# Attention beside a plain FFN, reordered per head, and an FFN end in an earlier form

## Chip, core and metric

The kernel runs on one core of one Trainium2 chip. The metric is device time in microseconds (us), the median of several runs. The kernel before takes 1391.65 us, median of three runs between 1391.4 and 1393.33 us. The profile is of one of these executions and has a span of 1389.6 us.

Five engines run in parallel, each through its own list of instructions in order: TensorE (PE in the profile; its weight loads are PEld), VectorE (DVE), ScalarE (ACT), GpSimd (POOL) and SyncE (SP), which here only starts transfers. An engine waits for another through semaphores.

## The reference

Attention with a threshold, then a two-layer network (FFN) with an ELU between its layers. Shapes: 8 batches, 8 heads, 576 positions, 64 values per head; the FFN has 4608 tokens, 512 inputs and 2048 hidden values. All in float32 on the chip.

```python
def _attn_ref(q, k, v, tau):
    scale = 1.0 / np.sqrt(q.shape[-1])
    scores = scale * np.matmul(q, k.transpose(0, 1, 3, 2))
    thresh = np.max(scores, axis=-1, keepdims=True) - tau
    scores = np.where(scores >= thresh, scores, -1000000000.0)
    scores = scores - np.max(scores, axis=-1, keepdims=True)
    attn = np.exp(scores)
    attn = attn / (np.sum(attn, axis=-1, keepdims=True) + 1e-09)
    return np.matmul(attn, v).astype(np.float32)

def _moe_ref(x, w_in, w_out):
    h = x @ w_in
    g = np.where(h > 0.0, h, np.exp(np.minimum(h, 0.0)) - 1.0)
    return (g @ w_out).astype(np.float32)
```

The weights arrive as float64, so the kernel first converts them by integer arithmetic, a piece of 128 x 512 at a time.

## The kernel before

Attention goes in steps: a step is 128 query rows of a pair of heads (or, every fifth step, the tails of both heads as one head's worth). For each step TensorE makes the scores; VectorE takes the row maxima; GpSimd makes from them the exponent's bias `nb` and the threshold `th`; ScalarE takes the exponentials `e`; VectorE masks them with the threshold and sums the rows in the same operation; GpSimd normalizes. Later TensorE transposes the weights and multiplies them with v.

The program has five parts in time: attention of the first batch (to about 107 us); attention beside the first plain FFN, with weight conversion (to about 240 us, of which conversion lasts to about 219 us); attention beside the rest of the plain FFN (to about 314 us); attention beside FFN groups that use seven products in place of eight (to about 1150 us), which come from sums of blocks; and the last two groups alone.

A piece of weights goes through five operations: `convert_rest` and `convert_abs` on ScalarE, `convert_top` and `convert_end` on VectorE, `convert_add` on GpSimd.

```python
    def convert_top(i):          # VectorE, lines 136 and 137
        ...
            nc.vector.tensor_scalar(top, hi, 3, 0x3FFFFFFF, ALU.logical_shift_left, ALU.bitwise_and)
            nc.vector.scalar_tensor_tensor(top, hi, 0xC0000000, top, ALU.bitwise_and, ALU.bitwise_or)
    def convert_add(i):          # GpSimd, line 143
        ...
            nc.gpsimd.tensor_tensor(top, top, staged[i][:, :, 0].bitcast(I32), ALU.add)
    def convert_end(i):          # VectorE, line 155
        ...
            nc.vector.scalar_tensor_tensor(pieces[i][1], mag, 1.125 * 2.0**-15, top, ALU.is_ge, ALU.mult)
```

The softmax of a step, for both heads at once:

```python
    def exponentials(pr, i, hs):
        ...
        nc.vector.tensor_reduce(st["mx"][:, cs], src[:, :, :, :HALF], axis=AX.XY, op=ALU.max)      # 248
        nc.gpsimd.tensor_scalar(st["nb"][:, cs], st["mx"][:, cs], nkeep, 1.0, ALU.mult, ALU.mult)  # 249
        nc.gpsimd.tensor_scalar(st["th"][:, cs], st["mx"][:, cs], 1.0, ntau, ALU.mult, ALU.add)    # 250
        for h in hs:
            e = att.tile([P, 2, HALF], FP32, name="e")
            nc.scalar.activation(e, st[h][:, :, :HALF], AF.Exp, bias=st["nb"][:, h : h + 1], scale=keep)
    def masks(pr, i, hs):
        ...
        for h in hs:
            nc.vector.scalar_tensor_tensor(wv, sc[:, :, :HALF], st["th"][:, h : h + 1], e, ALU.is_ge, ALU.mult,
                                           accum_out=sm[:, h : h + 1])                             # 265
        nc.vector.tensor_scalar(sm[:, cs], sm[:, cs], 1e-9, None, ALU.add)
        nc.vector.reciprocal(rs[:, cs], sm[:, cs])
    def normalize(pr, i, hs):
        for h in hs:
            nc.gpsimd.tensor_scalar(wv, wv, st["rs"][:, h : h + 1], 1.0, ALU.mult, ALU.mult)       # 274
```

In the second part the order is fixed by the program. One step of its loop, in which `now` are the two pieces of weights that are converted, and `ffn_halves(n)` puts n half units of the FFN on TensorE; `finish_units` puts their exponential (ScalarE), `minus` (GpSimd) and ELU (VectorE):

```python
            scores(*step, hs)
            if valued: out_values = values(...)
            parts = turn_parts(*steps[n - 1])
            for x in now[:1]: convert_top(x)
            finish_units(carried, slice(0, 2))
            for x in now[:1]: convert_add(x)
            copies = parts[0]()
            ...
            exponentials(*step, hs)
            finish_units(carried, slice(2, None))
            ...
            for x in now[:1]: convert_abs(x)
            share = SHARES[n % NB]
            after = ffn_halves(share[0])
            finish_units(after, ACT)
            for x in now[1:]: convert_top(x); convert_add(x); convert_abs(x)
            parts[1]()()
            second = ffn_halves(share[1])
            finish_units(second, ACT)
            if len(parts) > 2: parts[2]()()
            carried = ffn_halves(share[2])
            masks(*step, hs)
            finish_units(after + second, slice(1, 2))
            for x in now: convert_end(x)
            finish_units(after + second, slice(2, None))
            normalize(*step, hs)
            if i in (2, 3): (prep_q if i == 2 else prep_k)(pr + 1); ...
```

At the end, a unit of the first layer (`first_product`) is seven quarters on TensorE into three PSUM banks; ScalarE copies a bank (`w`, `u`, `s`), GpSimd and VectorE add, ScalarE takes two exponentials (the second after a lag), and VectorE makes the ELUs. `second_round` is the second layer, fourteen products of two quarters. A step of the agenda is placed at an estimated time, which fixes the order of instructions and nothing else.

Of the kernel before, what the change touches and what calls it, by code (L numbers as in the profile page):

```python
# [19 lines left out]
def kernel(  # L20
# [12 lines left out]
    P = 128  # L33
# [236 lines left out]
    def normalize(pr, i, hs):  # L270
        st = open_steps[pr, i]
        for h in hs:
            wv = st["w"][:, h * S : (h + 1) * S]
            nc.gpsimd.tensor_scalar(wv, wv, st["rs"][:, h : h + 1], 1.0, ALU.mult, ALU.mult)  # L274

# [303 lines left out]
    for name, bufs in (("s", 1), ("f", 2)):  # L579
        psum[name] = banks.enter_context(tc.tile_pool(name=f"ps_{name}", bufs=bufs, space=PSUM))  # L580
# [10 lines left out]
    with tc.manual_schedule():  # L591
# [3 lines left out]
        for n in range(per_seq, SWITCH):  # L595
# [13 lines left out]
            for x in now[:1]:  # L609
                convert_top(x)  # L610
            finish_units(carried, slice(0, 2))
            for x in now[:1]:
                convert_add(x)
# [3 lines left out]
            exponentials(*step, hs)  # L617
# [4 lines left out]
            for x in now[:1]:  # L622
                convert_abs(x)
            share = SHARES[n % NB]
            after = ffn_halves(share[0])
            finish_units(after, ACT)
            for x in now[1:]:
                convert_top(x)
                convert_add(x)
                convert_abs(x)  # L630
            parts[1]()()
            second = ffn_halves(share[1])
            finish_units(second, ACT)
            if len(parts) > 2:
                parts[2]()()
            carried = ffn_halves(share[2])
            masks(*step, hs)
            finish_units(after + second, slice(1, 2))
            for x in now:
                convert_end(x)  # L640
            finish_units(after + second, slice(2, None))
            normalize(*step, hs)
# [19 lines left out]
    apart.append(True)  # L662
    for name, bufs, stack in (("f", 3, ctx), ("s", 2, banks), ("t", 1, banks)):
        psum[name] = stack.enter_context(tc.tile_pool(name=f"ps_{name}2", bufs=bufs, space=PSUM))
# [81 lines left out]
    with tc.manual_schedule():  # L746
# [78 lines left out]
        def first_product(g, u):  # L825
# [69 lines left out]
            def elu(c):  # L895
# [21 lines left out]
                [(0.1, lambda: add(h(1, 1), 0, "s1")), (1.4 if attending[0] else 1.1, lambda: exp(1))],  # L917
# [147 lines left out]
        def ffn_quarters(n):  # L1065
            while n and (quarters or queue):
                if not quarters:
                    f, a = queue.popleft()
                    mine = f(*a)

                    if (f, a) == (second_round, (B, 1)):
                        mine = [mine[x] for x in (0, 2, 6, 1, 3, 4, 5)] + mine[7:]
                    quarters.extend(mine)
                p, posts = quarters.popleft()
                end = on_pe(QT, p)
                for lag, f in posts:
                    at(end + lag, f)
                n -= 1

        def max_of(pr, i, h):  # L1080
            st = open_steps[pr, i]
            nc.vector.tensor_reduce(st["mx"][:, h : h + 1], st[h][:, :, :HALF], axis=AX.XY, op=ALU.max)  # L1082

        def bound_of(pr, i, h):
            st = open_steps[pr, i]
            nc.gpsimd.tensor_scalar(st["th"][:, h : h + 1], st["mx"][:, h : h + 1], 1.0, ntau, ALU.mult, ALU.add)  # L1086

        def exp_of(pr, i, h):
            st = open_steps[pr, i]
            nc.scalar.mul(st["nb"][:, h : h + 1], st["mx"][:, h : h + 1], nkeep)  # L1090
            e = att.tile([P, 2, HALF], FP32, name="e")
            nc.scalar.activation(e, st[h][:, :, :HALF], AF.Exp, bias=st["nb"][:, h : h + 1], scale=keep)  # L1092
            st[h] = st[h], e

        def mask_of(pr, i, h):
            st = open_steps[pr, i]
            if h == 0:
                st["w"] = wpool[0].tile([P, 2 * S], FP32, name="w")
            sc, e = st.pop(h)
            wv = st["w"][:, h * S : (h + 1) * S].rearrange("p (a n) -> p a n", a=2)  # L1100
            nc.vector.scalar_tensor_tensor(wv, sc[:, :, :HALF], st["th"][:, h : h + 1], e, ALU.is_ge, ALU.mult,  # L1101
                                           accum_out=st["sm"][:, h : h + 1])

        def reciprocal_of(pr, i, hs):
            st = open_steps[pr, i]
            cs = slice(hs[0], hs[-1] + 1)
            nc.vector.tensor_scalar(st["sm"][:, cs], st["sm"][:, cs], 1e-9, None, ALU.add)
            nc.vector.reciprocal(st["rs"][:, cs], st["sm"][:, cs])  # L1108
# [67 lines left out]
        attending[0] = False  # L1176
        xs = [late["x"].tile([P, 2, CT], FP32, name=f"x{x}") for x in range(3)]
        for x, f in enumerate(sums_x(B - 1, xs)):
            at(clock[0] + 2.0 + 1.5 * x, f)
        while quarters or queue:  # L1180
            ffn_quarters(1)
            run_extra(0.9)
# [4 lines left out]

        banks.close()
        psum["f"] = ctx.enter_context(tc.tile_pool(name="ps_f3", bufs=5, space=PSUM))
        ends[:] = [bank() for _ in range(5)] + ends  # L1190
# [13 lines left out]
        nc.sync.dma_start(xts[B], xtail.rearrange("j p n -> p j n"))  # L1204
        xs = [qkp.tile([P, S], FP32, name="qT") for _ in range(2)] + [qkp.tile([P, TAIL + S], FP32, name="kT")]
# [49 lines left out]
```

## Time and profile before

| part of the time line (us) | TensorE busy | length |
|---|---|---|
| 106.8 to 218.7, attention with plain FFN and conversion | 95.95 us | 111.9 us |
| 218.7 to 239.6, the same without conversion | 20.88 us | 20.9 us |
| 239.6 to 314, attention with the rest of the plain FFN | 73.23 us | 74.4 us |
| 314 to 1150, attention with the groups of seven products | 829.01 us | 836.0 us |
| 1150 to 1389.6, the end | 227.10 us | 239.6 us |

Some durations of single instructions that are used below: a joint maximum of two heads 1.34 us, of one head 0.75 us; an exponential 0.83 us; a mask 0.82 us; a normalization 0.74 us when nothing else runs beside it, 0.86 us on average; `convert_add` 1.29 us; `convert_end` 0.68 us.

In a row of the time line the columns are start, length, engine, line, operation, what it writes and reads, and in brackets how long the engine stood idle before it and who released it. In the chain of waits each row is a piece of the chain of work that ended last.

### The profile page before, as it was taken

To read this page: it belongs to the slowest core of one execution; us is meant where nothing else is said; L and a number is where in the kernel's file an instruction comes from. 1 tells how busy PE (TensorE), PEld (TensorE's weight loads), DVE (VectorE), ACT (ScalarE), POOL (GpSimd) and SP (SyncE) were. 2 spreads that over 40 slices of the span, in tenths; PEclk is the share of its full clock that TensorE was granted. 3 is DMA by queue.
4 is the path that set the end of the run, shared out by engine and by line. 5 is a ranking of instruction groups with operands and counts; after the bars stand their busy time and mean duration, and the time that the engine had idled before them with its cause. 6 is when DMAs were issued, how large, how long until landed. Compare 5 with 4: busy or idle time off the path is not lost.

```text
span 1389.6 us, 21973 instructions
## 1 busy us (share of the span) xinstructions
PE 1336.3 (96%) x6566; PEld 988.0 (71%) x6566; DVE 1064.0 (77%) x2364; ACT 632.6 (46%) x1387; POOL 827.4 (60%) x1329
## 2 busy tenths in 40 slices
PE   6897989999999999999999999999999999999998
PEld 4454745747777777777777777777777777887886
DVE  6777885988888888888788878887888875444433
ACT  5566665225454445445453545363636351422421
POOL 5567774878657564757475747574766655423423
PEclk9899999999999999999999999999999999999999
DMA  5245452688898989798888888898889785321211
GB/s 114 57 88 146 136 147 44 189 245 239 236 261 234 264 218 256 197 281 231 235 229 259 238 235 235 242 251 220 236 229 273 211 238 146 115 69 54 92 57 31
DMA packets 316343, 259.83 MB, mean 187 GB/s; under 512 B 208320, under 2 KB 272320, under 8 KB 316224
## 3 DMA queue, kind: packets, MB, share of 16 engines
q1 hardware_dynamic: 316224, 258.42, 67.4%
q8 instruction: 53, 0.87, 0.3%
q14 instruction: 66, 0.54, 0.1%
HBM read 167.84 MB, written 90.51 MB: 186 GB/s over the span
## 4 chain that ended last, share of the span: by engine, by line
PE 75%; DVE 10%; ACT 6%; POOL 3%; issue 3%; DMA 2%; SPq 1%; DVEq 0%; POOLq 0%; ACTq 0%
PE f L999 28%; PE f L846 19%; PE sc L238 11%; PE pv L388 9%; PE f L475 3%; PE pv L384 2%; PE f L435 2%; ACT e L1092 2%; DVE w L265 2%; ACT e L253 1%; DVE mx L1082 1%; PE rt L277 1%; POOL wtop L143 1%; DVE wtop L137 1%; DVE mx L248 1%
## 5 line engine op out<-in xcount | busy, mean ns | idle before, releaser
L274 POOL TENSOR_SCALAR w<-w,rs 128x576 f32<-128x576 f32 x288 | 247.1, 864 | 108.3 <-DVE rs L1108 74.9
L1082 DVE TENSOR_REDUCE mx<-sc 128x1 f32<-128x576 f32 x207 | 147.9, 752 | 82.9 <-PE sc L238 82.9
L238 PE MATMUL sc<-kT,qT 64*128 64x288 f32 x1024 | 182.9, 440 | 21.1 <-DVE w L265 11.5
L348 DVE STREAM_TRANSPOSE x<-w 128x512 f32<-128x512 f32 (+1 forms) x350 | 182.6, 568 | 8.3 <-POOL w L274 8.3
L1090 ACT ACTIVATE nb<-mx,nkeep 128x1 f32<-128x1 f32 x207 | 61.4, 297 | 253.1 <-DVE mx L1082 253.1
L1092 ACT ACTIVATE e<-sc,nb,keep 128x576 f32<-128x576 f32 x207 | 172.2, 832 | 7.0
L1101 DVE SCALAR_TENSOR_TENSOR w<-sc,th,e 128x576 f32<-128x576 f32 x207 | 163.1, 810 | 8.7 <-ACT e L1092 0.4
L238 PEld LDWEIGHTS sc<-kT,qT 64*128 64x128 f32 x1024 | 100.8, 190 | 86.0 <-issue 52.1
L846 PE MATMUL f<-xt,sw 128*128 128x256 f32 x512 | 128.9, 389 | 0.5 <-DVE g L868 0.5
L846 PE MATMUL f<-xt,w_in_sb 128*128 128x256 f32 x512 | 125.2, 383 | 3.5 <-ACT w L860 3.3
L1086 POOL TENSOR_SCALAR th<-mx,ntau 128x1 f32<-128x1 f32 x207 | 55.0, 267 | 111.6 <-DVE mx L1082 111.4
L846 PE MATMUL f<-x,w_in_sb 128*128 128x256 f32 x448 | 109.0, 382 | 5.5 <-ACT g L913 5.5
L846 PEld LDWEIGHTS f<-xt,sw 128*128 128x128 f32 x512 | 93.3, 190 | 29.0 <-issue 13.5
L846 PEld LDWEIGHTS f<-xt,w_in_sb 128*128 128x128 f32 x512 | 95.4, 190 | 24.2 <-ACT w L860 6.2
L253 ACT ACTIVATE e<-sc,nb,keep 128x576 f32<-128x576 f32 x81 | 65.2, 831 | 103.9 <-POOL nb L249 103.1
L865 POOL TENSOR_TENSOR u<-u,w 128x256 f32<-128x256 f32 x64 | 48.8, 762 | 106.1 <-ACT u L860 106.1
L999 PE MATMUL f<-w_out_sb,s 128*128 128x256 f32 x448 | 109.4, 387 | 0.0
L999 PE MATMUL f<-w_out_sb,g 128*128 128x256 f32 x448 | 107.4, 383 | 1.9 <-ACT s L1004 1.9
L999 PE MATMUL f<-t,s 128*128 128x256 f32 x448 | 106.6, 380 | 0.3 <-POOL s L939 0.3
L846 PEld LDWEIGHTS f<-x,w_in_sb 128*128 128x128 f32 x448 | 84.1, 190 | 21.3 <-ACT g L913 10.3
L999 PEld LDWEIGHTS f<-w_out_sb,s 128*128 128x128 f32 x448 | 82.3, 190 | 23.0 <-issue 13.2
L999 PEld LDWEIGHTS f<-w_out_sb,g 128*128 128x128 f32 x448 | 83.8, 190 | 18.4 <-ACT ge L879 2.7
(162 smaller groups left out, 2579.3 us busy)
## 6 DMA issues: line engine op xcount, KB each, us to landing
there<-x SPq DMA_DIRECT2D x500, 144.0 KB, 4.2
wTb<-there SPq DMA_DIRECT2D x75, 576.0 KB, 4.7
wTa<-there SPq DMA_DIRECT2D x50, 576.0 KB, 4.4
sw<-win_sums SPq DMA_DIRECT2D x62, 384.0 KB, 4.8
t<-wout_sums SPq DMA_DIRECT2D x45, 512.0 KB, 5.3
qm<-in_q_dram SPq DMA_DIRECT2D x128, 72.0 KB, 4.3
vm<-in_v_dram SPq DMA_DIRECT2D x64, 128.0 KB, 4.0
wst<-in_moe_w_in_dram SPq DMA_DIRECT2D x16, 512.0 KB, 4.7
```

The source lines that it names most:

```text
L238: nc.tensor.matmul(scs[h][:, a, :HALF], qs[r], kT[r, k0 : k0 + HALF], start=True, stop=True)
L253: nc.scalar.activation(e, st[h][:, :, :HALF], AF.Exp, bias=st["nb"][:, h : h + 1], scale=keep)
L274: nc.gpsimd.tensor_scalar(wv, wv, st["rs"][:, h : h + 1], 1.0, ALU.mult, ALU.mult)
L348: nc.vector.transpose(x[:, :, c0 : c0 + nc_], src.rearrange("p (c g n) -> p g c n", c=nc_, n=T))
L388: nc.tensor.matmul(pv[h * D : (h + 1) * D, g0 * T : g1 * T], vm[:, h, c], wT[:, g0:g1, h * (NC + 1) + c], start=False, stop=(c == NC - 1), ...
L846: nc.tensor.matmul(loc["banks"][place], left[:, j], right[:, j], start=(begins and j == 0), stop=(j == 1), skip_group_check=True)
L999: nc.tensor.matmul(place(m), lhs, rhs, start=(begins and v == 0), stop=(v == RU - 1), skip_group_check=True)
L1082: nc.vector.tensor_reduce(st["mx"][:, h : h + 1], st[h][:, :, :HALF], axis=AX.XY, op=ALU.max)
L1086: nc.gpsimd.tensor_scalar(st["th"][:, h : h + 1], st["mx"][:, h : h + 1], 1.0, ntau, ALU.mult, ALU.add)
L1090: nc.scalar.mul(st["nb"][:, h : h + 1], st["mx"][:, h : h + 1], nkeep)
L1092: nc.scalar.activation(e, st[h][:, :, :HALF], AF.Exp, bias=st["nb"][:, h : h + 1], scale=keep)
L1101: nc.vector.scalar_tensor_tensor(wv, sc[:, :, :HALF], st["th"][:, h : h + 1], e, ALU.is_ge, ALU.mult, accum_out=st["sm"][:, h : h + 1])
```

## The change

The second part of the program, attention beside the first plain FFN, takes each head by itself: two score buffers of two banks each in place of one of four, a maximum, a threshold and an exponential for each head, with the bias `nb` made on ScalarE rather than on GpSimd. The helpers for that exist already for the later stage and move up unchanged. In the loop the maxima go ahead of the weight conversion, and masks and normalization ahead of the later FFN half units and their ELUs. The purpose is that exponentials don't wait behind a conversion on GpSimd.

The end of the FFN goes to an earlier form: the groups of attention are finished and all banks closed before the last two groups begin, with six new banks in place of five new and three kept; the sums of x for the last-but-one group are made there; the second exponential has a lag of 0.7 in place of 1.1; and the last round takes its quarters in the ordinary order.

```diff
@@ the loop of the second part @@
-    for name, bufs in (("s", 1), ("f", 2)):
+    apart.append(True)
+    for name, bufs in (("s", 2), ("f", 2)):
...
             parts = turn_parts(*steps[n - 1])
-            for x in now[:1]:
-                convert_top(x)
             finish_units(carried, slice(0, 2))
-            for x in now[:1]:
-                convert_add(x)
             copies = parts[0]()
             ...
-            exponentials(*step, hs)
+            for h in hs:
+                max_of(pr, i, h)
+                bound_of(pr, i, h)
+                exp_of(pr, i, h)
             finish_units(carried, slice(2, None))
             ...
             for x in now[:1]:
-                convert_abs(x)
+                convert_top(x)
+                convert_add(x)
             share = SHARES[n % NB]
             after = ffn_halves(share[0])
             finish_units(after, ACT)
+            for x in now[:1]:
+                convert_abs(x)
+            parts[1]()()
+            for h in hs:
+                mask_of(pr, i, h)
+            reciprocal_of(pr, i, hs)
+            finish_units(after, slice(1, 2))
+            normalize(*step, hs)
+            second = ffn_halves(share[1])
+            finish_units(second, ACT)
+            if len(parts) > 2:
+                parts[2]()()
+            finish_units(after, slice(2, None))
             for x in now[1:]:
                 convert_top(x)
                 convert_add(x)
                 convert_abs(x)
-            parts[1]()()
-            second = ffn_halves(share[1])
-            ...
             carried = ffn_halves(share[2])
-            masks(*step, hs)
-            finish_units(after + second, slice(1, 2))
-            for x in now:
+            finish_units(second, slice(1, 2))
+            for x in now[:1]:
                 convert_end(x)
-            finish_units(after + second, slice(2, None))
-            normalize(*step, hs)
+            finish_units(second, slice(2, None))
+            for x in now[1:]:
+                convert_end(x)
@@ the end @@
-                [..., (1.4 if attending[0] else 1.1, lambda: exp(1))],
+                [..., (1.4 if attending[0] else 0.7, lambda: exp(1))],
...
-                    if (f, a) == (second_round, (B, 1)):
-                        mine = [mine[x] for x in (0, 2, 6, 1, 3, 4, 5)] + mine[7:]
...
-        attending[0] = False
-        xs = [late["x"].tile([P, 2, CT], FP32, name=f"x{x}") for x in range(3)]
-        for x, f in enumerate(sums_x(B - 1, xs)):
-            at(clock[0] + 2.0 + 1.5 * x, f)
-        while quarters or queue:
+        ffn_quarters(len(quarters))
+        while queue:
             ffn_quarters(1)
-            run_extra(0.9)
+            ffn_quarters(len(quarters))
         until(1e9)
         run_extra(99)
+        attending[0] = False
         banks.close()
-        psum["f"] = ctx.enter_context(tc.tile_pool(name="ps_f3", bufs=5, space=PSUM))
-        ends[:] = [bank() for _ in range(5)] + ends
+        psum["f"] = ctx.enter_context(tc.tile_pool(name="ps_f3", bufs=6, space=PSUM))
+        ends[:] = [bank() for _ in range(6)]
...
         nc.sync.dma_start(xts[B], xtail.rearrange("j p n -> p j n"))
+        xs = [late["x"].tile([P, 2, CT], FP32, name=f"x{x}") for x in range(3)]
+        for f in sums_x(B - 1, xs):
+            f()
```

## The prediction

> **What bounds the kernel now.** I read the page's head first: TensorE is 96% busy over 1389.6 us, so a change can win only in the stretches where it is not. The stretches of the time line, cut at the stages of the program, say where those are (columns: length, then busy time of matmul, weight load, VectorE, ScalarE, GpSimd, then clock and DMA).
>
> ```profile
> 106.80:218.70 111.90, 95.95 (x469) 60.46 (x468) 95.21 (x172) 69.75 (x139) 81.16 (x88) 0.97 0.46 130
> 218.70:239.60 20.90, 20.88 (x106) 12.49 (x106) 8.72 (x19) 8.21 (x19) 6.80 (x13) 1.00 0.32 69
> 314.00:1150.00 836.00, 829.01 (x4214) 623.99 (x4213) 709.18 (x1614) 406.78 (x921) 533.30 (x887) 1.00 0.87 240
> 1150.00:1389.60 239.60, 227.10 (x1048) 193.11 (x1046) 107.80 (x204) 62.67 (x149) 86.27 (x114) 0.99 0.26 78
> ```
>
> The first row is the part that the change rewrites: 13 steps of attention beside the first plain FFN while weights are still converted. TensorE idles 111.9 - 95.95 = 16 us there and VectorE 16.7 us: neither is full, so a loop of waits sets the pace. The chain of waits shows that loop; here is one turn (columns: start, length, what).
>
> ```profile
> 116.87 1.29 POOL wtop L143
> 118.16 0.42 POOL nb L249
> ...
> 118.61 1.56 ACT e L253 x2
> ...
> 120.27 1.57 DVE w L265 x4
> ...
> 122.75 0.68 DVE w_in_sb L155
> 123.43 0.82 DVE wtop L136
> ...
> 124.28 1.12 DVE wtop L137
> ...
> 125.62 1.28 POOL wtop L143
> 126.90 0.42 POOL nb L249
> ```
>
> From one GpSimd addition (L143) to the next it takes 125.62 - 116.87 = 8.75 us: the bound nb stands behind the addition on GpSimd, the exponentials behind nb, the masks behind them, the two weight ends and the next top behind the masks on VectorE. The waits of VectorE, then of TensorE, in 106.8 to 219 (us in total, times, longest) show the holes:
>
> ```profile
> DVE w L265 <- ACT e L253: 12.5, 13, 1.1
> PE sc L238 <- DVE w L265: 8.2, 6, 4.5
> ```
>
> VectorE waits up to 1.1 us for the exponentials in each of 13 steps, and TensorE for the score banks that the masks free. The second row of the stretches has no hole at all (20.88 of 20.9): once conversion is over TensorE is full.
>
> **What the Trainium skill says.** "SBUF — State Buffer", section Who interferes with whom: VectorE and GpSimd share one pair of ports as an exclusive lock; VectorE takes it in a two-port mode, or for its second SBUF input against a GpSimd operation that reads SBUF; reductions, and operations with one SBUF input outside those modes, do not. The trace agrees in kind: L136 takes 0.42 us alone and 0.89 us beside a normalization, L137 0.69 and 1.11; a mask (one input in PSUM) keeps 0.82 us beside L143. It does not show whole blocking: L136, L137 and two normalizations of 0.74 us overlap in part. "Perfetto Trace Analysis", section Optimization Strategy: find the gap on the engine that should be full, and the instruction that releases it. The chain above does that. The PSUM page is not needed: the score buffers hold the same banks before and after.
>
> **The change, part one (attention beside the plain FFN).** It leaves the products as they are and reorders the loop. Removed per step: one joint maximum (1.34 us), one joint nb and th on GpSimd. Added: a maximum for each head (a pair took 1.42 us in the later attention stage), two nb on ScalarE (0.30 each), two th on GpSimd (0.27 each). Moved: maxima ahead of the first top; the first GpSimd addition behind th; normalization ahead of the second part of the FFN, with the second top and the second addition behind it.
>
> The exponential wait should vanish: after the first maximum (0.75) ScalarE needs 0.30 + 0.83, while VectorE has the second maximum and a top (0.7 + 1.2) to do. But the second addition now closes the step: maxima wait on VectorE behind the second weight end, that waits for the second addition, and that waits for normalization and the second top. I add the new loop for a step of two heads without an ELU: maxima 1.42, top 1.2 (0.5 + 0.7, GpSimd nearly idle), masks 1.57, sum and reciprocal 0.4, top beside normalization 2.0 (0.89 + 1.11), hand-over 0.23 (from L137's end at 125.39 to 125.62), addition 1.29, weight end 0.68. Sum 8.8 us, against 8.75 now. The wait of 1.1 us for exponentials is exchanged for one of about 1.1 us for the addition.
>
> With an ELU: it now stands between reciprocal and top (+0.65), and the top meets less of normalization (1.5 instead of 2.0, as at 169.5 to 171.1): 9.0 us. For the seven steps with ELUs (maxima from 125.31 to 189.01, 63.7 us now) I get six of 9.0, one of a single head 7.5 (0.75 + 1.2 + 0.84 + 0.35 + 0.65 + 1.5 + 0.23 + 1.29 + 0.68), four transposes of q or k that nothing hides (2.8), one carried and two second ELUs (1.8): 66.1 us, +2.4. The six others: two of 8.8 at the start against 17.3 us (+0.3), then one of a single head as now, then two against 17.5 us (+0.1), and the last, where only the masks' end counts for TensorE: 4.2 us after the maxima start (1.42 + 1.2 + 1.57) against 5.3 now (213.38 to 218.7), -1.1. Together **+1.7 us**. The 21 us behind it stay, TensorE being full.
>
> **Part two (end of the FFN, undone).** The version before drains into the last two groups with the sums of the next group already made, eight PSUM banks, a lag of 1.1 for the second exponential, and first the quarters of the last round that need no late ELU. Undone: (a) at 1181 us the five sums (0.68 each) start after the last final addition, which ends 0.7 us after TensorE now goes on, and the first new product also has a new wait for VectorE: about +1. (b) with a lag of 0.7 the second exponential (0.63) stands ahead of the copy w on ScalarE. TensorE waits for that copy five times in the end, 3.2 us in all, and in an undisturbed unit the copy is ready only 0.75 us early (1194.95 to 1195.71). Some units lose up to 0.6; the sums on VectorE come earlier in exchange: +1.5. (c) the last round runs into the late ELU after three products of 0.43 rather than six; 0.7 us of waiting becomes 1.9, of which 0.3 comes back: +1. Banks: six are enough for two units of three, no cost. Together **+3.5 us**.
>
> Sum: 1391.65 + 1.7 + 3.5 = 1396.9; I say 1396, since the first rival pulls down.
>
> **Rivals.** (1) The holes close and the stage becomes bound by work: VectorE has 95.2 us and TensorE 96 us in 111.9, plus 1 us of longer maxima; a stage of 100 to 104 us would give 8 to 12 us back, 1383 to 1388 with part two. For it: the exponential wait is surely gone, and the score banks come free a microsecond earlier in the step. Against it: the addition closes the loop on an in-order VectorE. (2) The two engines collide more: a weight end (two SBUF inputs) right beside the second addition, never so in the kernel before, could cost 0.6 us in each of 13 steps: +8, 1404. For it: normalization beside two weight ends and a top takes 2.44 us rather than 1.48. (3) TensorE's order decides: ELUs, exponentials and normalization may wait for FFN products in the steps with values. TensorE's work per step (7.4 us mean) leaves it early, so I give it little.
>
> **Range and chances.** Part one may be anything from -9 to +7, part two from 0 to +7; the ends are not likely together: 1385 to 1404. Two per cent is 28 us, more than the whole of TensorE's idle time in the stage, so within 2% is nearly sure; a loss of 28 us would need a stall in every step.
>
> **What would show it.** Right: the wait of the masks for exponentials gone, a new wait of about 1 us per step at the weight end (L155) for the GpSimd addition, a loop of 8.7 to 9.2 us, TensorE idle near 17 us in the stage, and a few us more idle after 1180. Wrong: VectorE above 93% busy in the stage and steps below 8.2 us (rival 1), additions longer than 1.3 us (rival 2), or ELUs waiting for ScalarE and TensorE (rival 3). For part two, the last 210 us should be 3 to 4 us longer; if they are not, the 6 banks and the lag cost nothing.

## The result and the profile after

The changed kernel takes **1402.15 us**, median of four runs, against 1391.53 us for the kernel before on the same chip: a ratio of 1.0074 with an interval of 1.0049 to 1.0099. Measured again beside other kernels (E5) it was 1398.84 us, a ratio of 1.0044 (1.0032 to 1.0056). So the loss is some 6 to 10 us; 1396 was predicted, with a range of 1385 to 1404. The total fell within the range, but the two halves of the sum did not come out as written: the attention loop loses about five times what was predicted, and the end of the FFN gains where a loss was predicted.

First the stretches of the time line of the changed kernel, cut at the same places as before except the last end (length, then busy time of matmul, weight load, VectorE, ScalarE, GpSimd, then clock, DMA share, GB/s):

```profile
106.80:218.70 111.90, 96.58 (x448) 61.24 (x449) 87.71 (x172) 71.49 (x152) 66.27 (x82) 0.94 0.53 132
218.70:239.60 20.90, 17.77 (x81) 9.50 (x80) 14.43 (x28) 11.16 (x24) 11.52 (x16) 1.00 0.02 6
314.00:1150.00 836.00, 829.87 (x4204) 620.95 (x4202) 711.84 (x1619) 403.05 (x908) 534.07 (x888) 1.00 0.87 240
1150.00:1397.20 247.20, 237.50 (x1100) 201.99 (x1096) 119.70 (x220) 70.28 (x167) 97.69 (x129) 0.99 0.28 86
```

In the first row VectorE does 7.5 us less in the same time: the loop is slower. (GpSimd does 15 us less, but in part because its work shrank: `nb` has moved to ScalarE.) The second row, which had no hole before, now holds VectorE work of the loop and 3.1 us of idle TensorE: conversion runs on to about 231 us. The third row is as before.

Next, one turn of the loop on VectorE, from the time line of the changed kernel (start, length, engine, line, operation, shapes; in brackets the idle time before it and who ended it). L278 are the two maxima, L136 and L137 a top, L155 a weight end; the first top, the masks, the reciprocal and the L136 of the second top are cut:

```profile
119.12 1.42 DVE L278 TENSOR_REDUCE mx<-sc 128x1 f32<-128x576 f32 x2
...
123.83 1.12 DVE L137 SCALAR_TENSOR_TENSOR wtop<-wst,wtop 128x512 uint32<-128x512 uint32 x1
124.87 0.68 DVE L155 SCALAR_TENSOR_TENSOR w_in_sb<-wst,wtop 128x512 f32<-128x512 f32 x1
127.38 0.69 DVE L155 SCALAR_TENSOR_TENSOR w_in_sb<-wst,wtop 128x512 f32<-128x512 f32 x1 [1.83 <-POOL wtop L143]
127.98 1.42 DVE L278 TENSOR_REDUCE mx<-sc 128x1 f32<-128x576 f32 x2
```

A turn takes 127.98 - 119.12 = 8.86 us. The second weight end stands idle for 1.83 us, and the next maxima, whose scores were long there, stand in order behind it. What GpSimd did in that time is in the chain of waits of the changed kernel (start, length, what):

```profile
123.65 1.34 POOL w L274 x2
...
126.04 1.31 POOL wtop L143
...
127.38 0.04 DVE w_in_sb L155
```

Two normalizations, then the addition. In the time line the two normalizations last 2.42 us, beside the second top and a weight end, where two with VectorE idle beside them take 1.47 (at 106.33 us). The waits of VectorE from 109 to 232 us (total, times, longest), and then of TensorE from 109 to 227 us and, in the last line, from 227 to 322 us, in the changed kernel:

```profile
DVE w_out_sb L155 <- POOL wtop L143: 10.9, 7, 1.8
DVE w_in_sb L155 <- POOL wtop L143: 6.1, 4, 1.8
DVE g L479 <- POOL g L475: 5.5, 4, 2.4
DVE w L297 <- ACT e L288: 0.9, 3, 0.4
```

```profile
PE rt L307 <- ACT xt L425: 7.1, 2, 3.6
...
PE sc L238 <- DVE w L297: 3.5, 4, 2.6
...
PE rt L307 <- ACT xt L425: 2.9, 1, 2.9
```

The wait of the masks for exponentials is all but gone (12.5 us to 0.9), and 17.0 us of waits for the addition take its place, with 5.5 us of ELUs (L479) that wait for their `minus` (L475).

Last the end. The waits of TensorE after 1160 us, in the kernel before and then in the changed one (L846 and L884 are the products of the first layer, L999 and L1037 those of the second, L860 and L898 the copies `w`, L1004 the copy `s`, L902 and L940 the ELU):

```profile
PE f L846 <- ACT w L860: 3.2, 5, 0.7
PE f L999 <- ACT s L1004: 2.8, 3, 0.9
PE f L999 <- DVE wTb L902: 0.7, 1, 0.7
```

```profile
PE f L1037 <- DVE wTb L940: 1.4, 1, 1.4
PE f L884 <- ACT w L898: 1.3, 4, 0.3
...
PE f L884 <- DVE ot L1055: 0.5, 1, 0.5
```

The copies `w`, which were to cost more, cost less, and the waits for the copies `s` on ScalarE are gone.

**Two measures from the traces** place a gain or a loss more sharply than whole times do. The first is the time of the 13 steps of attention beside the first plain FFN, from the start of the first maximum to that of the step after them: 220.87 - 108.01 us before, 232.11 - 109.46 us after. The second is the time from the first product of the groups with seven products to the end of the span: 1389.6 - 315.2 us before, 1397.2 - 326.9 us after. What lies between the two takes 93.7 to 95.2 us in all fourteen traces. What lies ahead of the first is the same program everywhere, yet its end, the first maximum, varies from 106.6 us (E11) to 111.0 us (E8), so a difference of a few us between whole times of two single traces says nothing.

| kernel | 13 steps, us | first group product to end, us | ratio of times (interval) |
|---|---|---|---|
| before | 112.9 | 1074.4 | 1 |
| changed | 122.7 | 1070.3 | 1.0074 (1.0049 to 1.0099) |
| E1 part one alone | 123.5 | 1074.1 | 1.0065 (1.0051 to 1.0079) |
| E2 part two alone | as before | 1069.6 | 0.9977 (0.9970 to 0.9984) |
| E3 lag of 0.7 alone | as before | 1068.4 | 0.9956 (0.9943 to 0.9969) |
| E4 values first | 128.2 | 1069.4 | 1.0066 (1.0054 to 1.0078) |
| E5 changed, again | as changed | 1069.3 | 1.0044 (1.0032 to 1.0056) |
| E6 weight end held | 109.2 | 1071.2 | 0.9939 (0.9925 to 0.9954) |
| E7 `nb` on ScalarE alone | 109.6 | 1073.5 | 0.9966 (0.9956 to 0.9976) |
| E8 `nb` and lag | 109.6 | 1066.9 | 0.9926 (0.9913 to 0.9938) |
| E9 `minus` earlier alone | as before | 1068.9 | 0.9968 (0.9957 to 0.9980) |
| E10 lag, quarters in order | as before | 1068.2 | 0.9964 (0.9952 to 0.9975) |
| E11 held, lag | 108.3 | 1066.9 | 0.9917 (0.9900 to 0.9934) |
| E12 held, values first, lag | 116.4 | 1066.9 | 0.9971 (0.9960 to 0.9982) |

"As before" and "as changed" mark kernels whose attention loop is the same program. The second measure repeats within 2 us for kernels with the same end: 1073.5 to 1074.4 for that of the kernel before (before, E1, E7), 1069.3 to 1071.2 for the changed one (changed, E2, E4, E5, E6), 1066.9 to 1068.4 for the old one with the lag of 0.7 (E3, E8, E11, E12).

### The profile page after: what moved, and what is told of

Read it like the earlier page. It is cut to its first block, busy times and chain, and to the rows that moved or that the text cites. A ratio compares the mean times of both kernels' runs of the same rounds, so it can differ in the third digit from the quotient of the medians.

```text
span 1397.2 us, 22000 instructions
## 1 busy us (share of the span) xinstructions
PE 1345.5 (96%) x6566; PEld 993.9 (71%) x6566; DVE 1066.8 (76%) x2374; ACT 641.2 (46%) x1414; POOL 819.3 (59%) x1328
## 4 chain that ended last, share of the span: by engine, by line
PE 72%; DVE 10%; ACT 5%; DMA 4%; POOL 4%; issue 3%; SPq 1%; DVEq 0%; POOLq 0%; ACTq 0%
PE f L1037 27%; PE f L884 19%; PE sc L238 11%; PE pv L418 8%; DMA there<-x 3%; DVE mx L278 3%; PE f L505 2%; PE pv L414 2%; ACT e L288 2%; POOL wtop L143 2%; DVE w L297 2%; PE f L465 2%; PE rt L307 1%; DMA wTa<-there 1%; POOL w L274 1%
## 5 line engine op out<-in xcount | busy, mean ns | idle before, releaser
L278 DVE TENSOR_REDUCE mx<-sc 128x1 f32<-128x576 f32 x234 | 167.0, 751 | 86.9 <-PE sc L238 86.9
L238 PE MATMUL sc<-kT,qT 64*128 64x288 f32 x1024 | 187.0, 440 | 16.6 <-DVE kT L200 8.1
L288 ACT ACTIVATE e<-sc,nb,keep 128x576 f32<-128x576 f32 x234 | 194.6, 832 | 7.8
L286 ACT ACTIVATE nb<-mx,nkeep 128x1 f32<-128x1 f32 x234 | 69.3, 296 | 274.9 <-DVE mx L278 274.9
L297 DVE SCALAR_TENSOR_TENSOR w<-sc,th,e 128x576 f32<-128x576 f32 x234 | 184.3, 811 | 12.4 <-ACT e L288 3.5
L282 POOL TENSOR_SCALAR th<-mx,ntau 128x1 f32<-128x1 f32 x234 | 63.1, 271 | 133.7 <-DVE mx L278 133.4
L884 PE MATMUL f<-xt,sw 128*128 128x256 f32 x512 | 129.0, 389 | 1.0 <-DVE ot L1055 0.5
L884 PE MATMUL f<-xt,w_in_sb 128*128 128x256 f32 x512 | 125.0, 383 | 1.7 <-ACT w L898 1.5
L884 PEld LDWEIGHTS f<-xt,sw 128*128 128x128 f32 x512 | 93.2, 190 | 29.9 <-issue 13.5
L884 PE MATMUL f<-x,w_in_sb 128*128 128x256 f32 x448 | 109.0, 382 | 5.5 <-ACT g L951 5.5
L884 PEld LDWEIGHTS f<-xt,w_in_sb 128*128 128x128 f32 x512 | 95.7, 190 | 22.1 <-ACT xs L430 4.6
L1037 PE MATMUL f<-w_out_sb,s 128*128 128x256 f32 x448 | 109.4, 387 | 0.0
L1037 PE MATMUL f<-t,s 128*128 128x256 f32 x448 | 106.7, 381 | 0.6 <-POOL s L977 0.6
L1037 PE MATMUL f<-w_out_sb,g 128*128 128x256 f32 x448 | 107.2, 382 | 0.0
L884 PEld LDWEIGHTS f<-x,w_in_sb 128*128 128x128 f32 x448 | 84.1, 190 | 21.3 <-ACT g L951 10.3
L1037 PEld LDWEIGHTS f<-w_out_sb,s 128*128 128x128 f32 x448 | 82.3, 190 | 23.0 <-issue 13.2
L1037 PEld LDWEIGHTS f<-w_out_sb,g 128*128 128x128 f32 x448 | 83.9, 190 | 15.9 <-ACT ge L917 3.5
L1037 PEld LDWEIGHTS f<-t,s 128*128 128x128 f32 x448 | 84.0, 190 | 14.3 <-POOL s L977 3.4
```

The source lines that it names most:

```text
L238: nc.tensor.matmul(scs[h][:, a, :HALF], qs[r], kT[r, k0 : k0 + HALF], start=True, stop=True)
L884: nc.tensor.matmul(loc["banks"][place], left[:, j], right[:, j], start=(begins and j == 0), stop=(j == 1), skip_group_check=True)
L1037: nc.tensor.matmul(place(m), lhs, rhs, start=(begins and v == 0), stop=(v == RU - 1), skip_group_check=True)
```

## The experiments

All times are medians beside runs of the kernel before on the same chip.

### E1 and E2: each part alone

E1 has the changed attention loop and the end of the kernel before. E2 is the opposite.

```diff
 E1:  loop as changed;   end as before (lag 1.1, five new banks, sums of x early, quarters of the last round reordered)
 E2:  loop as before;    end as changed (lag 0.7, six new banks, sums of x late, quarters in order)
```

> The new order of the attention loop alone, with the end of the FFN as in the kernel before. Theory from the two traces (part one loses 11.7 us, part two gives 4.1 back): ratio about 1.008, some 1402 to 1404 us; stretch up to the first product of the seven-product groups 10 to 12 us longer than before, the end as before. Rival (my recorded prediction: part one +1.7, part two +3.5): about 1393 us, ratio 1.001.

> The old form of the FFN end alone, with the loop as in the kernel before. Theory: 1387 us, ratio 0.997, waits of TensorE for the copies w and s after 1150 us falling from 6 us to under 2. Rival (my prediction): 1395 us, ratio 1.0025.

E1: 1401.28 us. The loop alone loses 0.65%, 9.0 us (7.1 to 11.0). E2: 1388.94 us. The end alone gains 0.23%, 3.2 us (2.2 to 4.2). The two multiply to 1.0042; E5 measures 1.0044 for both. So there is no sign that the parts act on one another, and the loss is all of part one.

### E5: the changed kernel again

> The changed kernel once more, beside the next three on one chip. If parts one and two add up (1.0065 and 0.9977), the ratio is 1.004; if they don't, it stays near 1.0074.

1398.84 us, 1.0044 (1.0032 to 1.0056), beside 1.0074 (1.0049 to 1.0099) in the first measurement; the intervals overlap. Part of what the one profile of the changed kernel shows is not of the change: its first maximum of the stage comes 1.45 us later than before, and E1, with the same program up to there, has only 0.4, E5 itself 2.8.

### E3: only the lag

```diff
-                [..., (1.4 if attending[0] else 1.1, lambda: exp(1))],
+                [..., (1.4 if attending[0] else 0.7, lambda: exp(1))],
```

> The kernel before with one number changed, the lag of the second exponential 0.7 in place of 1.1 after the attention stage. Theory: the lag is what gains in part two, through exponential, minus and ELU that come earlier and let the sums on VectorE end before the additions: the waits for copies w and s (6.0 us before) fall under 2 us and the time to about 1386.5 us, ratio 0.9965, a little better than part two as a whole, whose other edits lose about 1 us. Rival: the kept banks and the order of the last quarters matter and the lag does not: 1391 us, ratio 1.000; or my prediction, +1.5 us.

1386.52 us, 0.9956: a gain of 6.1 us (4.3 to 7.9), more than that of the whole of part two. The waits of TensorE after 1160 us in E3:

```profile
PE f L846 <- ACT w L860: 1.2, 4, 0.3
PE f L999 <- POOL s L939: 0.3, 1, 0.3
PE f L999 <- DVE ot L1019: 0.2, 1, 0.2
```

The second exponential ahead of the copy `w` does not delay that copy. What it brings forward is seen in the time line of VectorE; first a second-column ELU (L902) of the kernel before, then GpSimd's `minus` (L893) and the same ELU in E3:

```profile
1197.16 1.20 DVE L902 SCALAR_TENSOR_TENSOR g<-ge,g 128x512 f32<-128x512 f32 x1 [1.75 <-ACT g L913]
```

```profile
1196.82 0.62 POOL L893 TENSOR_SCALAR ge<-ge 128x512 f32<-128x512 f32 x1 [2.45 <-ACT ge L879]
...
1197.47 1.20 DVE L902 SCALAR_TENSOR_TENSOR g<-ge,g 128x512 f32<-128x512 f32 x1 [0.54 <-POOL ge L893]
```

VectorE's idle time before that ELU falls from 1.75 to 0.54 us. (The first row names the copy L913 as what ended the wait. It ends at 1197.14 us, but `minus` ends at 1197.13 us there, and in E3 the ELU starts before that copy: `minus` is what it waits for.) Behind it stand, in order, the sums for the second layer and the additions on which the next bank depends. But the lag moves two things: the exponential on ScalarE, and with it the place of `minus` in GpSimd's order (ahead of the addition `u + w` rather than behind it). E9 parts them.

### E9: only the place of `minus`

```diff
-                    at(now[0] + 1.6, minus)
+                    at(now[0] + (1.6 if attending[0] else 1.0), minus)
```

The lag stays 1.1. The only instructions whose order differs from the kernel before are GpSimd's: in the trace `minus` has changed places in 12 units of the end, and VectorE and ScalarE have their old order.

> The kernel before with its lag of 1.1 kept; only the minus of the second exponential goes ahead of the addition u+w on GpSimd in the end (it is placed 1.0 rather than 1.6 after its exponential). It tells which of two effects of the lag of 0.7 gains the 5 us. If the place of minus in GpSimd's order is the cause: ELUs of the second column wait 0.5 us or less, the waits of TensorE for the copies s vanish (2.8 us before), ratio 0.995 to 0.997. If it is the earlier exponential on ScalarE (0.4 us earlier in each unit): the exponential isn't there yet, GpSimd waits in order with u+w behind it, and the time stays or rises: 1.000 to 1.004. I lean to 0.998, a part of it.

1387.84 us, 0.9968: a gain of 4.5 us (2.8 to 6.0). In E9 the waits of TensorE after 1160 us, and GpSimd and VectorE at the same ELU:

```profile
PE f L999 <- ACT s L1004: 0.8, 3, 0.4
...
PE f L846 <- ACT w L860: 0.4, 1, 0.4
```

```profile
1195.15 0.62 POOL L893 TENSOR_SCALAR ge<-ge 128x512 f32<-128x512 f32 x1 [2.72 <-ACT ge L879]
1195.73 0.72 POOL L865 TENSOR_TENSOR u<-u,w 128x256 f32<-128x256 f32 x1
```

```profile
1195.80 1.20 DVE L902 SCALAR_TENSOR_TENSOR g<-ge,g 128x512 f32<-128x512 f32 x1 [0.81 <-POOL ge L893]
```

So most of the gain of the lag comes with the exchange of two neighbours on GpSimd, `minus` (0.62 us) and `u + w` (0.72 us), 12 times. E9 expected 0.998, a part of the gain, with 0.995 to 0.997 if the place of `minus` were the cause: the measured 0.9968 is in the latter, though the waits for the copies `s` do not vanish (0.8 us) and the ELU still waits 0.81 us rather than 0.5. By the second measure it is 5.5 us (1074.4 to 1068.9), of the 6.0 that E3 has.

### E10: the lag without the new order of the last round

```diff
-                    if (f, a) == (second_round, (B, 1)):
-                        mine = [mine[x] for x in (0, 2, 6, 1, 3, 4, 5)] + mine[7:]
```

(on top of E3)

> The kernel before with the lag of 0.7 and with the quarters of the last round in their ordinary order; draining and banks stay as before. Part two as a whole was 0.9977 and the lag alone 0.9956, so the other edits lose some 3 us. If the order of the quarters makes them, as step (c) of the prediction has it in part (+1 us): ratio 0.9963 to 0.998, with a wait of TensorE for the late ELU of 1.4 us or more. If the drained banks and late sums make them: 0.9956.

1387.36 us, 0.9964 (0.9952 to 0.9975), beside 0.9956 (0.9943 to 0.9969) for E3: not told apart. The trace has the wait for the late ELU as expected:

```profile
PE f L999 <- DVE wTb L902: 1.4, 1, 1.4
```

Yet the time from the first product is 1068.2 us, against 1068.4 in E3: the order of the quarters is worth less than these runs can tell. Part two loses something else against the lag alone: 0.9977 against 0.9956, or, by the means of the second measure, 1070.0 us over five kernels against 1067.3 over four. That is left to the draining of the queue, the late sums and the banks, which were not tried one by one.

### E4: copies of the values ahead of the exponentials

The changed kernel showed a wait that the prediction had not named: TensorE's transposes wait for a copy of values (L425) that stands on ScalarE behind the exponentials. E4 moves the copies ahead.

```diff
-            if not valued: copies()
+            if valued: out_values()
+            copies()
             for h in hs: max_of(pr, i, h); bound_of(pr, i, h); exp_of(pr, i, h)
-            if valued: out_values(); copies()
```

> The changed kernel with the copies of a value product put ahead of the step's exponentials on ScalarE. Theory: TensorE's wait for the copy xt at a transpose (10.0 us in the changed kernel, in three places) vanishes; only the last of the three, 2.9 us, stands on the path, since the loop of weight conversion absorbs the others: 3 us less than the changed kernel, ratio about 1.0055 against before. Rival, in which TensorE's order bounds the new loop: 7 to 10 us less, ratio 1.000 to 1.0025. A third: exponentials now wait for the values and the loop grows: more than 1.0074.

1401.33 us, 1.0066 (1.0054 to 1.0078): no gain. The waits of E4 from 109 to 232 us, of TensorE and of VectorE:

```profile
PE sc L238 <- DVE w L297: 12.2, 10, 2.6
...
DVE w_out_sb L155 <- POOL wtop L143: 9.1, 6, 1.8
DVE w L297 <- ACT e L288: 6.1, 9, 2.7
```

The wait for the copy is gone; the exponentials are late instead, the masks wait for them, and TensorE waits for the score banks that the masks free (3.5 us before this edit). The 13 steps take 128.2 us, 5.5 more than in the changed kernel, so one wait was exchanged for a longer one: that is the third expectation, a loop that grows, although 1.0066 does not pass the 1.0074 that was named for it. The waits at the weight end (L155) are nearly as long as they were.

### E6: the second weight end held back

This is the run on which the theory stands or falls. The theory: the second weight end closes the loop, because the next maxima stand in order behind it. The rival: the work of the loop sets its length (VectorE and GpSimd in one another's way), and moving the weight end moves the wait. E6 does the same work and puts the second weight end behind the next step's maxima.

```diff
             for h in hs: max_of(pr, i, h); bound_of(pr, i, h); exp_of(pr, i, h)
+            while held: convert_end(held.pop()); load_w(4)
             ...
-            for x in now[1:]: convert_end(x)
+            held.extend(now[1:])
```

> The changed kernel with the second weight end of each step held back until the next step's maxima and exponentials are out. Theory (the second GpSimd addition closes the loop through that weight end): the wait of VectorE for wtop (17 us in all) goes, a two-headed step without an ELU falls from 8.87 us to about 7.5 us, the stage ends 10 to 14 us earlier than in the changed kernel, and the time is 1387 to 1392 us, ratio 0.997 to 1.000. Rival (collisions of VectorE and GpSimd set the step): the step stays over 8.4 us and the ratio over 1.004. Second rival (TensorE stalled behind the copy xt sets it): waits of TensorE for xt stay near 10 us and the ratio above 1.004.

1383.34 us, 0.9939 (0.9925 to 0.9954): 8.5 us below the kernel before, where the changed kernel is above it. The waits of VectorE from 109 to 219 us in E6, and then the stretch of the stage:

```profile
DVE g L479 <- POOL g L475: 5.7, 4, 2.4
DVE w L297 <- ACT e L288: 1.3, 3, 0.7
DVE w_out_sb L155 <- POOL wtop L143: 1.0, 2, 0.5
DVE w_in_sb L155 <- POOL wtop L143: 0.5, 1, 0.5
```

```profile
106.80:218.70 111.90, 103.71 (x502) 64.76 (x502) 99.00 (x191) 77.97 (x166) 80.07 (x90) 0.97 0.50 130
```

17.0 us of waits at the weight end become 1.5; the turns without ELUs take 7.87 to 8.30 us (the longest has its maxima at 115.13 and 123.43 us) rather than 8.86; the 13 steps take 109.2 us rather than 122.7. In the stretch TensorE does 502 products, against 469 before and 448 after. The 13 steps alone, in the kernel before, the changed one and E6, show what differs:

```profile
108.01:220.87 112.86, 96.89 (x476) 61.00 (x478) 97.34 (x176) 69.53 (x138) 82.16 (x89) 0.97 0.45 127
109.46:232.11 122.65, 107.39 (x498) 66.56 (x496) 97.33 (x189) 76.83 (x162) 74.08 (x88) 0.94 0.46 118
107.98:217.14 109.16, 100.97 (x486) 63.08 (x486) 97.44 (x189) 76.79 (x162) 78.57 (x88) 0.97 0.51 132
```

VectorE is busy for 97.3 to 97.4 us in all three: what the changed kernel loses and E6 wins is idle time of VectorE, 15.5, 25.3 and 11.7 us. GpSimd works longer in E6 than in the changed kernel, and the loop is shorter all the same. So the rival falls. TensorE's granted clock was lower in the changed loop (0.94), but VectorE waits for TensorE there only once, for 2.9 us ahead of the first maximum. The expectation was a turn of about 7.5 us and 0.997 to 1.000; the turns are longer than that, and the whole gained more. It goes most of the way to the first rival of the prediction, the closing of the holes (which had named steps below 8.2 us and VectorE above 93%; it is 99.00 of 111.9 us, 88%), as soon as the loop is cut open.

### E7 and E8: only the bias on ScalarE, then with the lag

E7 is the kernel before with its joint maxima and its order of the loop; only `nb` goes from GpSimd to ScalarE.

```diff
-        nc.gpsimd.tensor_scalar(st["nb"][:, cs], st["mx"][:, cs], nkeep, 1.0, ALU.mult, ALU.mult)
+        nc.scalar.mul(st["nb"][:, cs], st["mx"][:, cs], nkeep)      # in the plain FFN only
```

> The kernel before with only the bias nb moved from GpSimd to ScalarE in the attention beside the plain FFN, nothing reordered. Theory (the order on GpSimd, nb behind an addition, closes the old loop): the masks' wait for exponentials (12.5 us) falls under 4 us, steps fall from 8.75 to about 7.8 us, and the time to about 1384 us, ratio 0.994. Rival (the old loop is bound by VectorE's work and collisions, or TensorE takes over at once): ratio 0.998 to 1.000.

> The last one with the lag of 0.7 as well, a version meant to beat both kernels. The two lie in different stages and should add: about 1378 us, ratio 0.990; if the first gives nothing, 0.9956.

E7: 1387.48 us, 0.9966, a gain of 4.7 us (3.3 to 6.1), smaller than expected: a wait of the masks under 4 us, turns of 7.8 us and 0.994 were named. The turns without ELUs take 8.4 us, and the masks still wait for exponentials; that both exponentials still follow one maximum of 1.34 us for two heads may be why, but no run tries it. From 106.8 to 219 us in E7, where the kernel before has 12.5 us:

```profile
DVE w L268 <- ACT e L256: 7.9, 11, 1.0
```

But `nb` no longer stands behind the addition, and the 13 steps take 109.6 us rather than 112.9. So the purpose of the change, that exponentials should not stand behind a conversion on GpSimd, was sound: this one line has it without the new loop. E8 adds E3's lag: 1381.80 us, 0.9926, where about 0.990 was expected; the product of E7 and E3 is 0.9922. The parts add.

### E11 and E12: the changed loop, held, with the lag; and the values first

E11 is E6's loop with the end of the kernel before and the lag of 0.7. E12 adds E4's edit.

```diff
 E11: E6's loop  +  (1.4 if attending[0] else 0.7, lambda: exp(1)), rest of the end as before
 E12: E11        +  out_values() and copies() ahead of max_of, bound_of, exp_of
```

> The changed attention loop with the second weight end held until behind the next maxima (as in the run where it was held), the end of the kernel before, and the lag of 0.7 in it. If the parts add: 0.9939 / 0.9977 x 0.9956 = 0.992, 1380.4 us, about that of the bias on ScalarE with the lag (0.9926). Waits at the weight end below 2 us in all, first product of the groups near 312 us, last stretch 5 us shorter than before.

> The same, and in steps with values ScalarE's copies of the values go ahead of the exponentials. With the weight end last in the step (values first, run e4) this gained nothing, as the masks then waited for the exponentials. If that wait was set by the late maxima, it is gone now and the 3 us wait for the copies as well: 0.990. If the exponentials behind the values are late by themselves: 0.992 to 0.994 and masks that wait for exponentials by 0.6 us and more a step.

E11: **1379.63 us, 0.9917** (0.9900 to 0.9934), as the parts had it (0.992). It beats both kernels; E8 at 0.9926 is not told apart from it. E12: 1387.78 us, 0.9971. The values first lose 7 to 8 us here; the 13 steps take 8.1 us longer (116.4 against 108.3). The waits of VectorE from 109 to 219 us in E12:

```profile
DVE w L297 <- ACT e L288: 7.7, 11, 4.2
DVE g L479 <- POOL g L475: 7.2, 5, 2.4
```

In E11 the first of these is 0.4 us. Of the two outcomes that were written down, the second comes closer: the masks wait for exponentials by 0.7 us on average in 11 steps, so exponentials behind the values are late by themselves. But the time is worse than the 0.992 to 0.994 that were named for it, and why is open. TensorE's granted clock in the stage was 0.92 in E12 and 0.97 in E11 (and 0.91 in E4), so a part of the difference may be that.

## Why the prediction came out as it did

**Right.** The wait of the masks for exponentials disappears. A wait at L155 for GpSimd's addition takes its place; the turn without ELUs is 8.86 us where 8.8 was summed. TensorE idles 15.3 us in the stage where 17 was named. The reasoning that the second addition closes the loop on an in-order VectorE is shown by E6, which changes nothing but the place of that weight end and of the transfer issued behind it. ("PSUM — Partial Sum Buffer", section Engine vs sequencer instructions, calls the queues of ScalarE, VectorE and GpSimd strictly first in, first out; 1.83 us of idle VectorE with its next maxima ready agree.)

Two of these numbers are near in part by luck. The sum has the second addition released by the second top, after 2.0 us and a hand-over of 0.23. In the trace that top takes 0.40 and 1.12 us and ends at 124.95 us, and the addition starts only at 126.04 us, behind the two normalizations: the loop closes through GpSimd's queue. And the 17 us of idle TensorE were reckoned for a loop of nearly the old length. The loop became 9.8 us longer, yet over the 13 steps TensorE idles 15.3 us, against 16.0 before: it is busy for longer instead, 107.4 us with 498 products against 96.9 us with 476.

**Part one was mis-sized: +1.7 us said, +9.0 us (7.1 to 11.0) measured in E1.** By the prediction's own stretches, in the trace of the changed kernel against before:

| stretch of the sum | said | measured |
|---|---|---|
| two steps at the start, 109.46 to 127.98 us, against 17.3 us | +0.3 | 18.5: +1.2 |
| seven steps with ELUs, 127.98 to 197.72 us, against 63.7 us | +2.4 | 69.7: +6.0 |
| single head and two more, 197.72 to 222.56 us, against 24.4 us | +0.1 | 24.8: +0.5 |
| last step, 222.56 to 232.11 us, against 7.5 us | -1.1 | 9.6: +2.1 |

- The ELU term. A plain ELU step, 157.70 to 167.27 us, takes 9.57 us rather than 9.0. Three collisions are in it, the last of them the one that the second rival named; the time line of VectorE and GpSimd of the changed kernel has them.

```profile
161.68 0.64 DVE L303 TENSOR_SCALAR sm<-sm 128x2 f32<-128x2 f32 x1
...
161.69 0.62 POOL L475 TENSOR_SCALAR g<-g 128x512 f32<-128x512 f32 x1
...
163.02 0.69 DVE L136 TENSOR_SCALAR wtop<-wst 128x512 uint32<-128x512 uint32 x1
163.75 1.11 DVE L137 SCALAR_TENSOR_TENSOR wtop<-wst,wtop 128x512 uint32<-128x512 uint32 x1
...
165.00 1.63 POOL L143 TENSOR_TENSOR wtop<-wtop,wst 128x512 int32<-128x512 int32 x1 [0.68 <-POOL w L274]
```

  The addition of 1e-9 (L303), 0.17 us elsewhere, starts beside `minus` and ends with it; the top takes 1.84 us (163.02 to 164.86) beside normalization, where 1.5 was summed; the GpSimd addition takes 1.63 us beside a weight end rather than 1.29. That is +0.47, +0.34 and +0.34, of which the other terms of the sum, most of them a little shorter, take some 0.6 back. All three lie on the path of this step: VectorE has no gap from the maxima to the end of the top, the addition follows at 165.00 us and the weight end at 166.66. Over the stage three such L303 and six such L143 stand in the trace, some 1.4 + 2.1 = 3.5 us by their lengths; no run takes only these away. So the sign of the second rival, additions over 1.3 us, did appear, but at 0.3 to 0.4 us in six steps rather than 0.6 in 13.

- The second and carried ELUs were put at 1.8 us together. Here their `minus` stands on GpSimd behind normalization and the second addition, and VectorE waits for it by up to 2.4 us, 5.5 us in four waits. A step with such an ELU (167.27 to 177.93 us) takes 10.66 us, 1.8 over the 8.86 of a turn without ELUs. This is the third rival, in GpSimd's queue rather than in TensorE's.

- The last step. The sum took the masks' end for what counts, as TensorE's next scores wait for it; that held (the last mask ends 3.95 us after the maxima start, where 4.2 was summed, and the scores start at 225.83 us). But the held-up weight ends stand ahead of the next maxima, their exponentials stand ahead of the copy of values on ScalarE, and TensorE waits:

```profile
235.47 0.63 PE L307 MATMUL rt<-ident,w 128*128 128x128 f32 x4 [2.86 <-ACT xt L425]
```

  "The 21 us behind it stay, TensorE being full" was the failing sentence: from the last mask's end to the first product of the groups with seven products it takes 100.4 us (226.51 to 326.91) rather than 96.5 (218.66 to 315.18), and 2.9 of these 3.9 us are the wait above. (The table's +2.1 is counted to the next maximum, so a part of this stands in it.) E4 and E12 show that moving the copy ahead does not mend it.

**Part two had the wrong sign: +3.5 us said, -3.2 us (-4.2 to -2.2) measured in E2.** The step that failed is (b), the lag, put at +1.5; alone it gives -6.1 us (E3). The danger that was named, the copy `w` behind the exponential, did not come: its waits fall from 3.2 to 1.2 us. "The sums on VectorE come earlier in exchange" was the right thought, and it was given too little weight; E9 shows that the larger part of it hangs on the place of `minus` on GpSimd. Of the other steps, (a), a later transition at +1, shows as the 0.5 us wait for `ot` at the transition; (c), the late ELU, as 1.4 us of waiting rather than 0.7, at +1 said, and too little for E10 to tell. Both waits have the right sign: all edits of part two other than the lag together turn 0.9956 into 0.9977, about +3 us against +2 said. Six banks show no wait of their own.

The two errors, +7.3 us and -6.7 us, nearly cancel in the sum. That the total was near is luck: a total within its range says little for the terms.

## What to carry to other kernels

When a chain of engines in order closes into a loop, ask for the last instruction of the turn what stands behind it without needing it: moving one weight end behind the next maxima turned a loss of 6 to 10 us into a gain of 8. The place of a short instruction in another engine's queue can matter: `minus`, 0.62 us, ahead of its neighbour in 12 units gained 4.5 us. And where a change bundles several edits, run them singly: the lag and the bias on ScalarE gained 6.1 and 4.7 us alone, and the whole lost.

## What the runs showed of the hardware

A VectorE operation of two elements per partition on 128 rows (L303) took 0.60 to 0.64 us, rather than 0.17, in all three cases of the changed kernel where it started with a GpSimd operation of 0.61 or 0.62 us, and ended with it. In E6 two more started 0.11 and 0.19 us after such an operation and took 0.55 and 0.45 us, again to its end. That agrees with "SBUF — State Buffer", section Who interferes with whom, where VectorE in a mode of two ports and GpSimd hold the shared pair for a whole instruction; that L303 runs in such a mode is not shown by a trace. Larger operations lose less than their whole overlap: the addition L143 grows from 1.29 to between 1.62 and 1.69 us beside a weight end of 0.68. In the kernel before none of its 25 additions in the stage took over 1.30 us; in the changed one six did.
